# Attention keys in chunks of 128 with shared blocks for the left-over keys, in a fused attention and MLP kernel

## The chip, the cores and the metric

The kernel runs on one core of a Trainium2 chip. The metric is the device time of one execution in microseconds (us); a lower one is better. A run of one kernel is a handful of executions, of which one is profiled.

The engines are called as in the profile: PE is TensorE's matrix multiplies, PEld its weight loads, DVE is VectorE, ACT is ScalarE, POOL is GpSimd, SP is SyncE. POOLq and SPq are the sequencers of the two that issue transfers. L12 is line 12 of the kernel in question, so one piece of work has other line numbers in other kernels. In a row of the profile `x4` is a number of instructions, and what stands in brackets is the time for which the engine stood idle before the row, with what ended that idleness.

## The reference

```python
batch, n_heads, seq, head_dim = (8, 12, 448, 64)      # q, k, v

scores = scale * np.matmul(q, k.transpose(0, 1, 3, 2))
m = np.max(scores, axis=-1, keepdims=True)
e = np.exp(scores - m)
attn = e / (np.sum(e, axis=-1, keepdims=True) + np.exp(-m) + 1e-09)
attn_out = np.matmul(attn, v)

x = attn_out.transpose(0, 2, 1, 3).reshape(B * S, H * D)   # 3584 x 768
h = x @ w_in                                               # w_in: 768 x 2048
g = 0.5 * h * (1.0 + erf(h / sqrt(2)))
return g @ w_out                                           # w_out: 2048 x 768
```

## The kernel before

Two heads form a pair: 6 pairs in each of 8 batches, 48 pairs. The keys of a head (448) are cut in four chunks of 112. For a pair TensorE computes transposed scores, two heads side by side on 64 rows each; ScalarE takes the exponential; VectorE adds the four chunks for the denominators; TensorE multiplies by the values and sums the denominators with a matrix of ones. The MLP of one batch runs between the attention of the next, in units that the steps below are handed.

PSUM, where TensorE's results land, has two buffers of two banks for scores and four single banks for everything else:

```python
re_pool = ctx.enter_context(tc.tile_pool(name="re_pool", bufs=2))
et_pool = ctx.enter_context(tc.tile_pool(name="et_pool", bufs=2))
...
ps_st = ctx.enter_context(tc.tile_pool(name="ps_st", bufs=2, space=bass.MemoryType.PSUM))
ps_bank = ctx.enter_context(tc.tile_pool(name="ps_bank", bufs=4, space=bass.MemoryType.PSUM))
```

The queries and keys must reach TensorE transposed. For batches 2 to 7 a transfer does it. VectorE first copies the loaded rows into a staging buffer `re`, which has two instances here; then a DMA transpose reads it:

```python
def transpose_on_dma(b, w):                       # w: 0 queries, 1 keys
    ...
    re = re_pool.tile([PS, NPAIR, NJ, 2, D], FP16, name="re")
    for e in range(2):
        nc.vector.tensor_copy(out=re[:, :, :, e, :], in_=src[:, :, e])
    nc.sync.dma_start_transpose(out=..., in_=re...)
```

This is a step of the steady part, and what a step fetches (`r` counts the six steps of a batch):

```python
def step(s, first, second):
    closing = s % NPAIR == 0
    if s < NSTEP:
        scores(s, 0)                  # two of four chunks
    for f in first:                   # MLP
        f()
    ...
    if s < NSTEP:
        scores(s, 1)                  # the other two
    if not closing:
        denominators(s - 1)
        values(s - 1)
        reciprocals(s - 1)            # logarithm and exponential on ScalarE
    for f in second:                  # MLP
        f()
    ...
    if not closing:
        normalize(s - 1)              # VectorE

# after each step
if r == 0 and b + 2 < B:
    load_v(b + 2)
if r in (1, 2) and b + 2 < B:
    transpose_on_dma(b + 2, r - 1)
if r == 3 and b + 3 < B:
    load_qk(b + 3)
if r == last:
    gelu_window(b, f1)
```

The loads are issued by GpSimd in program order, each as soon as its buffer is free: `load_v(b + 2)` needs the values of batch b to have been used for the last time, and `load_qk`, which stands behind it in the same queue, waits with it. `gelu_window` runs the rest of layer 1 and all gelus between two loads of ScalarE's tables. MLP results leave their banks through VectorE's copies to `hbuf` and `osb`, or inside the window through ScalarE.

The softmax here doesn't subtract the row's maximum and nothing guards it: scores larger than these inputs give would overflow.

Of the kernel before, what the change touches and what calls it, by code (L numbers as in the profile page):

```python
# [19 lines left out]
def kernel(  # L20
# [16 lines left out]
    PS = S // NJ  # L37
    NPAIR = H // 2
# [16 lines left out]
    re_pool = ctx.enter_context(tc.tile_pool(name="re_pool", bufs=2))  # L55
    qt_pool = ctx.enter_context(tc.tile_pool(name="qt_pool", bufs=2))
    v_pool = ctx.enter_context(tc.tile_pool(name="v_pool", bufs=2))
    et_pool = ctx.enter_context(tc.tile_pool(name="et_pool", bufs=2))
    sum_pool = ctx.enter_context(tc.tile_pool(name="sum_pool", bufs=1))
# [6 lines left out]
    ps_st = ctx.enter_context(tc.tile_pool(name="ps_st", bufs=2, space=bass.MemoryType.PSUM))  # L66
    ps_bank = ctx.enter_context(tc.tile_pool(name="ps_bank", bufs=4, space=bass.MemoryType.PSUM))
# [16 lines left out]
    raw_t, v_t, qt_t = {}, {}, {}  # L84

    def load_heads(pool, name, tiles, key, src, h0=0, h1=H):

        if key not in tiles:
            tiles[key] = pool.tile([PS, H, NJ, D], FP16, name=name)
        nc.gpsimd.dma_start(  # L90
            out=tiles[key][:, h0:h1],
            in_=src[key[0]].rearrange("h (p j) d -> p h j d", j=NJ)[:, h0:h1],
        )

    def load_qk(b, *heads):
        for w, src in (("q", q), ("k", k)):
            load_heads(raw_pool, f"raw{w}", raw_t, (b, w), src, *heads)

    def load_v(b, *heads):
        load_heads(v_pool, "vn", v_t, (b,), v, *heads)  # L100
# [18 lines left out]
    load_qk(0, 0, 2)  # L119
    ident = const.tile([PS, PS], FP16, name="ident")  # L120
    make_identity(nc, ident)
    ones = const.tile([PS, D], FP16, name="ones")
# [6 lines left out]
    load_qk(0, 2, 6)  # L129
    load_v(0, 0, 6)  # L130
    load_qk(0, 6, 12)
    load_v(0, 6, 12)
    load_qk(1)
    for i in range(4):
        load_w_in(i, 4)
    load_v(1)
    for i in range(4):
        load_w_out(i, 4)


    def alloc_qt(b):
        qt_t[b] = qt_pool.tile([P, 2, NPAIR, NJ, PS], FP16, name="tqk")

    def transpose_on_pe(b, c):
        tp = ps_bank.tile([P, 2, NJ, PS], FP16, name="bank")
        for w in range(2):
            src = raw_t[b, "qk"[w]]
            for j in range(NJ):
                for e in range(2):
                    nc.tensor.transpose(  # L150
                        tp[e * D:(e + 1) * D, w, j, :], src[:, 2 * c + e, j, :], ident
                    )
        nc.vector.tensor_copy(out=qt_t[b][:, :, c], in_=tp)  # L153

    def transpose_on_dma(b, w):
        if w == 0:
            alloc_qt(b)
        src = raw_t[b, "qk"[w]].rearrange("p (c e) j d -> p c e j d", e=2)
        re = re_pool.tile([PS, NPAIR, NJ, 2, D], FP16, name="re")
        for e in range(2):  # L160
            nc.vector.tensor_copy(out=re[:, :, :, e, :], in_=src[:, :, e])
        nc.sync.dma_start_transpose(
            out=qt_t[b][:, w].rearrange("p c j s -> p (c j) s"),
            in_=re.rearrange("p c j e d -> p (c j e d)"),
        )


    et_t, sum_t, xt_t = {}, {}, {}

    def scores(g, half):  # L170
        b, c = divmod(g, NPAIR)
        qt, kt = qt_t[b][:, 0], qt_t[b][:, 1]
        if half == 0:
            et_t[g] = et_pool.tile([PS, NJ, 2, S], FP16, name="et")
        for j in (2 * half, 2 * half + 1):
            st = ps_st.tile([P, 2, 512], FP32, name="st")
            for e in range(2):
                r = slice(e * D, (e + 1) * D)
                nc.tensor.matmul(  # L179
                    st[0:PS, e, 0:S], kt[r, c, j, :],  # L180
                    qt[r, c].rearrange("p j s -> p (j s)"), start=True, stop=True,
                )
            nc.scalar.activation(  # L183
                out=et_t[g][:, j], in_=st[0:PS, :, 0:S], func=AF.Exp,
                bias=expb[0:PS], scale=scale,
            )

    def presum(g, part):

        et = et_t[g]  # L190
        if part == 0:
            sum_t[g] = [sum_pool.tile([PS, 2, 2, S], FP16, name="t2"), None]
        t2 = sum_t[g][0]
        nc.vector.tensor_tensor(  # L194
            out=t2[:, part], in0=et[:, 2 * part], in1=et[:, 2 * part + 1], op=ALU.add)
        if part == 1:
            sum_t[g] = sum_pool.tile([PS, 2, S], FP16, name="ksum")
            nc.vector.tensor_tensor(out=sum_t[g], in0=t2[:, 0], in1=t2[:, 1], op=ALU.add)  # L198

    po_t, den_t, rec_t = {}, {}, {}  # L200

    def values(g):
        b, c = divmod(g, NPAIR)
        et = et_t.pop(g)
        po_t[g] = ps_bank.tile([P, 512], FP32, name="bank")
        for j in range(NJ):
            for e in range(2):
                nc.tensor.matmul(  # L208
                    po_t[g][e * D:(e + 1) * D, 0:S], v_t[b,][:, 2 * c + e, j, :], et[:, j, e, :],
                    start=(j == 0), stop=(j == NJ - 1),  # L210
                )

    def denominators(g):
        den_t[g] = ps_bank.tile([P, 512], FP32, name="bank")
        for e in range(2):
            nc.tensor.matmul(  # L216
                den_t[g][e * D:(e + 1) * D, 0:S], ones, sum_t[g][:, e, :], start=True, stop=True,
            )

    def reciprocals(g):  # L220
        rec_t[g] = rec_pool.tile([P, S], FP32, name="rec")
        nc.scalar.activation(out=rec_t[g], in_=den_t.pop(g)[:, 0:S], func=AF.Ln, bias=oneb, scale=1.0)  # L222
        nc.scalar.activation(out=rec_t[g], in_=rec_t[g], func=AF.Exp, scale=-1.0)  # L223
# [8 lines left out]
    def attend(g):  # L232
        denominators(g)
        values(g)
        reciprocals(g)
        normalize(g)

# [3 lines left out]
    NBURST = 10  # L241
# [8 lines left out]
    def layer1(b, fc, direct=False):  # L250
        ph = ps_bank.tile([P, 512], FP32, name="bank")
        for m in range(MCH):
# [3 lines left out]
            )  # L256
        if direct:
# [22 lines left out]
    def layer2_items(b):  # L280
# [7 lines left out]
        for gt, g0, where in tiles:  # L288
            osb_h = {}

            def unit(nh, u, gt=gt, g0=g0, where=where, osb_h=osb_h):
                if nh == 0 and u == 0:
                    osb_h[0] = osb_pool.tile([P, DM], FP32, name="osb")
                if u == 0:
                    osb_h[1] = ps_bank.tile([P, 512], FP32, name="bank")
                osb, po = osb_h[0], osb_h[1]
                n0 = nh * NHW
                for fc in range(u * FCH // 2, (u + 1) * FCH // 2):
# [4 lines left out]
                if u == 0:  # L303
                    return
# [7 lines left out]
            for nh in range(NH):  # L312
                for u in range(2):
                    items.append(lambda nh=nh, u=u, unit=unit: unit(nh, u))
# [6 lines left out]
    def start_step(s):  # L321

        scores(s, 0)
        if s >= 2:
            normalize(s - 2)
        if s + 1 < NPAIR:
            transpose_on_pe(0, s + 1)
        if s >= 1:
            denominators(s - 1)
        presum(s, 0)  # L330
        scores(s, 1)
        if s >= 1:
            values(s - 1)
            reciprocals(s - 1)
        for c in {3: (0,), 4: (1, 2), 5: (3, 4)}.get(s, ()):
            transpose_on_pe(1, c)
        presum(s, 1)

    def step(s, first, second):

        closing = s % NPAIR == 0
        if s < NSTEP:
            scores(s, 0)
        for f in first:
            f()
        if s < NSTEP:
            presum(s, 0)
        if closing:
            attend(s - 1)
        if s < NSTEP:  # L350
            scores(s, 1)
        if not closing:
            denominators(s - 1)
            values(s - 1)
            reciprocals(s - 1)
        for f in second:
            f()
        if s < NSTEP:
            presum(s, 1)
        if not closing:  # L360
            normalize(s - 1)

    def mlp1(b, f0, f1):
        return [lambda fc=fc: layer1(b, fc) for fc in range(f0, f1)]
# [6 lines left out]
    def gelu_window(b, n):  # L371

        load_table(SET_GELU)
        for f in take(len(l2)):
            f()
        if b == 0:
# [13 lines left out]
    transpose_on_pe(0, 0)  # L390
# [3 lines left out]
    load_qk(2)  # L394
    scores(NPAIR, 0)
    normalize(NPAIR - 2)
    transpose_on_pe(1, NPAIR - 1)
    presum(NPAIR, 0)
    denominators(NPAIR - 1)
    values(NPAIR - 1)  # L400
    reciprocals(NPAIR - 1)
    normalize(NPAIR - 1)
    scores(NPAIR, 1)
    for f in mlp1(0, 0, 2):
        f()
    presum(NPAIR, 1)

    for s in range(NPAIR + 1, NSTEP + 1):
        b, r = divmod(s - 1 - NPAIR, NPAIR)

        if b == 0:
            f0, f1, last = 2, 6, 0
        else:
            half = (NBURST if b > 1 else NBURST - 2) // 2
            f0, f1, last = half * r, half * (r + 1), 1
        if r <= last:
            step(s, mlp1(b, f0, f0 + 2), mlp1(b, f0 + 2, f1))
        else:

            left = len(l2) - (0 if b == 0 else 2 if b % 2 == 0 else 4)  # L420
            n = left if r == NPAIR - 1 else max(2, left // (NPAIR - r))
            if r == last + 1:
                n = 4
            step(s, take(n // 2), take(n - n // 2))
        if r == 0 and b + 2 < B:
            load_v(b + 2)
        if r in (1, 2) and b + 2 < B:
            transpose_on_dma(b + 2, r - 1)
        if r == 3 and b + 3 < B:
            load_qk(b + 3)  # L430
        if r == last:
            gelu_window(b, f1)
# [38 lines left out]
```

## Time and profile before

| | before |
|---|---|
| median (lowest to highest), 3 runs | 444.81 us (443.97 to 445.48) |
| profiled span, granted TensorE clock | 442.8 us, 0.995 |
| share busy: PE, ACT, DVE, POOL | 95%, 72%, 45%, 7% |

The prediction shows the main lines of this profile. A timeline gives start, duration, engine, line, operation. The page's row of the TensorE clock has one digit for each fortieth of the span (9 is full speed):

```profile
PEclk9989999999999999999999999999999999999999
```

```profile
123.29 1.02 DVE L161 COPY re<-rawk 112x1536 f16<-112x1536 f16 x2
124.34 3.26 SPq L162 DMA_TRANSPOSE tqk<-re  x1
...
136.04 0.94 POOL L90 DMA_DIRECT2D vn<-in_v_dram  x1 [45.09 <-PE bank L208]
```

VectorE fills the staging buffer without waiting. The second transpose of the batch is issued at 124.34, and the loads of the next values only at 136.04, after both transposes are over. No load runs beside a transpose here (of the twelve in this kernel only the first two, issued together, have any beside them: 296 packets), and in the packets' records a transpose of 2688 packets then lasts 3.4 us, its first packet 1.2 us after the issue.

### The profile page before, as it was taken

To read this page: it belongs to the slowest core of one execution; us is meant where nothing else is said; L and a number is where in the kernel's file an instruction comes from. 1 tells how busy PE (TensorE), PEld (TensorE's weight loads), DVE (VectorE), ACT (ScalarE), POOL (GpSimd) and SP (SyncE) were. 2 spreads that over 40 slices of the span, in tenths; PEclk is the share of its full clock that TensorE was granted. 3 is DMA by queue.
4 is the path that set the end of the run, shared out by engine and by line. 5 is a ranking of instruction groups with operands and counts; after the bars stand their busy time and mean duration, and the time that the engine had idled before them with its cause. 6 is when DMAs were issued, how large, how long until landed. Compare 5 with 4: busy or idle time off the path is not lost.

```text
span 442.8 us, 6605 instructions
## 1 busy us (share of the span) xinstructions
PE 419.7 (95%) x2720; PEld 208.3 (47%) x2720; DVE 198.3 (45%) x351; ACT 317.8 (72%) x426; POOL 32.5 (7%) x43
## 2 busy tenths in 40 slices
PE   3878999999999999999999999999999999999995
PEld 2344444444444454445444454444544455445562
DVE  1567416664165532657154641566346560440021
ACT  3989988978787757969787678887788685854300
POOL 8312100020002000020002000000000000000000
PEclk9989999999999999999999999999999999999999
DMA  8999999696148840493443931460414101111022
GB/s 98 196 207 205 210 199 201 141 164 101 21 99 126 134 98 19 114 145 45 99 98 63 198 60 39 98 99 0 99 44 92 36 1 36 37 36 37 0 73 71
DMA packets 75118, 42.50 MB, mean 96 GB/s; under 512 B 34128, under 2 KB 71504, under 8 KB 75088
## 3 DMA queue, kind: packets, MB, share of 16 engines
q0 software_dynamic: 37968, 22.81, 36.7%
q1 hardware_dynamic: 37120, 19.27, 18.5%
q8 instruction: 21, 0.34, 0.3%
q14 instruction: 9, 0.07, 0.1%
HBM read 45.61 MB, written 11.01 MB: 128 GB/s over the span
## 4 chain that ended last, share of the span: by engine, by line
PE 76%; ACT 17%; issue 2%; DVE 1%; DMA 1%; POOL 1%; POOLq 0%
PE bank L253 34%; PE bank L299 23%; ACT et L183 14%; PE st L179 8%; PE bank L208 8%; PE bank L216 3%; ACT L70 2%; DMA rawk<-in_k_dram 1%; PE bank L150 1%; ACT rec L222 1%; ACT gt_odd L259 0%; ACT gt_even L259 0%; DVE ksum L198 0%; DVE tqk L153 0%; ACT rec L223 0%
## 5 line engine op out<-in xcount | busy, mean ns | idle before, releaser
L183 ACT ACTIVATE et<-st,expb 112x896 f16<-112x896 f32 x192 | 181.5, 1004 | 56.8 <-PE st L179 56.4
L253 PE MATMUL bank<-xt,w_in_sb 128*128 128x448 f16 x768 | 151.2, 353 | 0.0
L305 DVE COPY osb<-bank 128x384 f32<-128x384 f32 x56 | 31.2, 557 | 174.6 <-PE bank L299 174.6
L253 PEld LDWEIGHTS <-w_in_sb 128*128 128x128 f16 x768 | 72.9, 98 | 74.2 <-issue 9.4
L299 PE MATMUL bank<-w_out_sb,gt_odd 128*128 128x384 f16 x512 | 88.0, 326 | 0.0
L179 PE MATMUL st<-tqk 64*112 64x448 f16 x384 | 64.7, 385 | 7.8 <-ACT et L183 5.5
L299 PE MATMUL bank<-w_out_sb,gt_even 128*128 128x384 f16 x384 | 68.5, 327 | 0.0
L299 PEld LDWEIGHTS <-gt_odd 128*128 128x128 f16 x512 | 48.1, 98 | 38.5 <-issue 8.3
L194 DVE TENSOR_TENSOR t<-et 112x896 f16<-112x896 f16 x96 | 59.4, 618 | 5.9 <-ACT et L183 5.3
L263 DVE COPY hbuf<-bank 128x448 f32<-128x448 f32 x64 | 39.9, 624 | 39.0 <-PE bank L253 39.0
L299 PEld LDWEIGHTS <-gt_even 128*128 128x128 f16 x384 | 34.9, 98 | 32.1 <-issue 10.1
L208 PE MATMUL bank<-et,vn 112*64 112x448 f16 x384 | 45.5, 360 | 0.0
L179 PEld LDWEIGHTS <-tqk 64*112 64x112 f16 x384 | 21.7, 127 | 46.4 <-issue 44.5
L259 ACT ACTIVATE gt_odd<-bank 128x448 f16<-128x448 f32 (+1 forms) x64 | 25.3, 401 | 20.2 <-PE bank L253 19.9
L222 ACT ACTIVATE rec<-bank,oneb 128x448 f32<-128x448 f32 x48 | 30.7, 639 | 2.1 <-PE bank L216 2.1
L229 DVE TENSOR_TENSOR xt<-bank,rec 128x448 f16<-128x448 f32 x48 | 29.7, 619 | 5.0 <-ACT rec L223 5.0
L198 DVE TENSOR_TENSOR ksum<-t 112x896 f16<-112x896 f16 x48 | 30.0, 625 | 1.8
L223 ACT ACTIVATE rec<-rec 128x448 f32<-128x448 f32 x48 | 27.7, 577 | 1.5
L208 PEld LDWEIGHTS <-vn 112*64 112x64 f16 x384 | 21.6, 111 | 12.4 <-issue 2.2
L259 ACT ACTIVATE gt_even<-bank 128x384 f16<-128x384 f32 x28 | 13.7, 490 | 17.6 <-PE bank L253 17.6
L90 POOL DMA_DIRECT2D vn<-in_v_dram x9 | 8.1, 903 | 236.4 <-PE bank L208 184.4
L216 PE MATMUL bank<-ksum,ones 112*64 112x448 f16 x96 | 18.5, 380 | 4.5 <-DVE ksum L198 4.5
(24 smaller groups left out, 119.3 us busy)
## 6 DMA issues: line engine op xcount, KB each, us to landing
rawq<-in_q_dram POOLq DMA_DIRECT2D x7, 672.0 KB, 11.7
rawk<-in_k_dram POOLq DMA_DIRECT2D x7, 672.0 KB, 14.1
vn<-in_v_dram POOLq DMA_DIRECT2D x7, 672.0 KB, 8.1
w_in_sb<-in_moe_w_in_dram POOLq DMA_DIRECT2D x4, 768.0 KB, 22.8
w_out_sb<-in_moe_w_out_dram POOLq DMA_DIRECT2D x4, 768.0 KB, 29.9
out_dram<-osb SPq DMA_DIRECT2D x8, 336.0 KB, 2.8
out_dram<-osb SPq DMA_DIRECT2D x8, 288.0 KB, 2.7
out_dram<-osb SPq DMA_DIRECT2D x8, 240.0 KB, 3.3
```

The source lines that it names most:

```text
L179: nc.tensor.matmul(st[0:PS, e, 0:S], kt[r, c, j, :], qt[r, c].rearrange("p j s -> p (j s)"), start=True, stop=True,)
L183: nc.scalar.activation(out=et_t[g][:, j], in_=st[0:PS, :, 0:S], func=AF.Exp, bias=expb[0:PS], scale=scale,)
L194: nc.vector.tensor_tensor(out=t2[:, part], in0=et[:, 2 * part], in1=et[:, 2 * part + 1], op=ALU.add)
L198: nc.vector.tensor_tensor(out=sum_t[g], in0=t2[:, 0], in1=t2[:, 1], op=ALU.add)
L208: nc.tensor.matmul(po_t[g][e * D:(e + 1) * D, 0:S], v_t[b,][:, 2 * c + e, j, :], et[:, j, e, :], start=(j == 0), stop=(j == NJ - 1),)
L216: nc.tensor.matmul(den_t[g][e * D:(e + 1) * D, 0:S], ones, sum_t[g][:, e, :], start=True, stop=True,)
L222: nc.scalar.activation(out=rec_t[g], in_=den_t.pop(g)[:, 0:S], func=AF.Ln, bias=oneb, scale=1.0)
L253: nc.tensor.matmul(ph[:, 0:S], w_in_sb[:, m, fc * P:(fc + 1) * P], xt_t[b][:, m, :], start=(m == 0), stop=(m == MCH - 1),)
L259: nc.scalar.activation(out=dst[:, 0, :], in_=ph[:, c0:c1], func=AF.Gelu)
L263: nc.vector.tensor_copy(out=h_t[b][:, fc, :], in_=ph[:, 0:S])
L299: nc.tensor.matmul(po[:, 0:NHW], gt[:, fc, g0:g0 + P], w_out_sb[:, fc, n0:n0 + NHW], start=(fc == 0), stop=(fc == FCH - 1),)
L305: nc.vector.tensor_copy(out=osb[:, n0:n0 + NHW], in_=po[:, 0:NHW])
```

## The change

Its intent: 448 keys are three chunks of 128 and 64 left over. The left-over keys of the two heads of a pair go into one block-diagonal block of 128 (zeros elsewhere), so that they take one full-array matmul. All row-tiled score matmuls of a pair stand in one burst, the left-over ones in the middle of MLP work that uses the array in full as they do, and the values follow three pairs behind, next to the denominators. This cuts the changes between ways of tiling the array, and work on ScalarE.

```diff
-    re_pool = ctx.enter_context(tc.tile_pool(name="re_pool", bufs=2))
+    left_pool = ctx.enter_context(tc.tile_pool(name="left_pool", bufs=1))
+    re_pool = ctx.enter_context(tc.tile_pool(name="re_pool", bufs=1))
...
-    et_pool = ctx.enter_context(tc.tile_pool(name="et_pool", bufs=2))
-    sum_pool = ctx.enter_context(tc.tile_pool(name="sum_pool", bufs=1))
+    et_pool = ctx.enter_context(tc.tile_pool(name="et_pool", bufs=4))
+    sum_pool = ctx.enter_context(tc.tile_pool(name="sum_pool", bufs=2))
...
-    ps_st = ... bufs=2 ...
-    ps_bank = ... bufs=4 ...
+    ps_st = ... bufs=3 ...
+    ps_bank = ... bufs=2 ...
...
+    def scores_left(g):
+        b, c = divmod(g, NPAIR)
+        qt, _, kl = qt_views(b, c)
+        st = ps_st.tile([P, 2, 512], FP32, name="st")
+        nc.tensor.matmul(st[:, 0, 0:S], kl, qt, start=True, stop=True)
+        exps(g, NK, st)
...
-    def step(s, first, second):
...
+    def step(s, work):
+        if s - 3 in et_t:
+            values(s - 3)                 # left-over values first, full array
+        if s - 2 in sum_t:
+            denominators(s - 2)
+            log_den(s - 2)
+        if s < NSTEP:
+            for j in range(NK):           # NK = 3
+                scores(s, j)
+        if s - 2 in rec_t:
+            exp_den(s - 2)
+        if s - 3 in po_t:
+            normalize(s - 3)
...
+        for i, f in enumerate(work):
+            f(mid=(lambda: scores_left(s)) if i == 0 and s < NSTEP else None)
...
+    def fetch(b, r):
         if r == 0 and b + 2 < B:
             load_v(b + 2)
-        if r in (1, 2) and b + 2 < B:
-            transpose_on_dma(b + 2, r - 1)
+            load_left(vl, v, b + 2)
+        if r in (0, 1) and b + 2 < B:
+            transpose_on_dma(b + 2, r)
         if r == 3 and b + 3 < B:
-            load_qk(b + 3)
+            load_q(b + 3)
+            load_k(b + 3)
+            load_left(kl_raw, k, b + 3)
```

Cut here are the loads in their new shapes (key and value rows as 3 x 64 elements a partition), the sums in six halves instead of three, the start-up in its new order, and the counts of MLP units for each step. `re_pool` goes from two buffers to one, and `fetch` starts the transposes one step earlier.

## The prediction

> **What bounds the kernel now.** I began with the table of engines and the chain that ended last.
>
> ```profile
> span 442.8 us, 6605 instructions
> PE 419.7 (95%) x2720; PEld 208.3 (47%) x2720; DVE 198.3 (45%) x351; ACT 317.8 (72%) x426; POOL 32.5 (7%) x43
> PE 76%; ACT 17%; issue 2%; DVE 1%; DMA 1%; POOL 1%; POOLq 0%
> L183 ACT ACTIVATE et<-st,expb 112x896 f16<-112x896 f32 x192 | 181.5, 1004 | 56.8 <-PE st L179 56.4
> L179 PE MATMUL st<-tqk 64*112 64x448 f16 x384 | 64.7, 385 | 7.8 <-ACT et L183 5.5
> ```
>
> TensorE is the bound, and ScalarE's exponentials (L183) hold it up in places. A busy 95% hides how full the array is, because overlapping records are counted. So I went to the timeline of TensorE in one stretch of steady work.
>
> ```profile
> 199.67 1.86 PE L253 MATMUL bank<-xt,w_in_sb 128*128 128x448 f16 x9
> 201.46 0.58 PE L179 MATMUL st<-tqk 64*112 64x448 f16 x4
> 201.98 0.38 PE L216 MATMUL bank<-ksum,ones 112*64 112x448 f16 x2
> 202.19 0.92 PE L208 MATMUL bank<-et,vn 112*64 112x448 f16 x8
> 203.05 3.58 PE L253 MATMUL bank<-xt,w_in_sb 128*128 128x448 f16 x18
> 206.46 2.76 PE L299 MATMUL bank<-w_out_sb,gt_even 128*128 128x384 f16 x16
> ```
>
> Eighteen L253 matmuls fill 203.05 to 206.46, 189 ns each, and L299 follows at once: both use the full array. But nine of them from 199.67 would end at 201.37, and the scores (L179, two row tiles of 64) start at 201.46, 0.09 late. Scores run two at a time, 0.193 a pair, so four should end at 201.85; the denominators (L216, column tiles) start at 201.98. Eight values (L208) are four pairs of 0.187 and should end at 202.94; L253 starts at 203.05. Every change between full, row-tiled and column-tiled use costs about 0.09 to 0.13 us.
>
> Summing all start-to-start gaps of successive matmuls in the trace gives this account of the span: 4.4 before the first matmul, 378.0 of streaming (189 ns for 448 columns, 163 for 384, a tiled pair counted once), 233 changes of tiling worth 21.9, 32.8 of other waiting, 5.7 after the last start. From 61.1 us to 398.2 (steady work) there are 201 changes (18.9 us) and 14.9 of other waiting, 11.3 of it between one score matmul and the next. Before 40.4 us the other waiting is 17.6. The steps with little MLP work show the score wait:
>
> ```profile
> 180.14 0.59 PE L179 MATMUL st<-tqk 64*112 64x448 f16 x4
> 180.58 3.83 ACT L183 ACTIVATE et<-st,expb 112x896 f16<-112x896 f32 x4 [0.23 <-PE st L179]
> 182.07 0.87 PE L179 MATMUL st<-tqk 64*112 64x448 f16 x4
> 184.30 0.64 ACT L222 ACTIVATE rec<-bank,oneb 128x448 f32<-128x448 f32 x1
> 184.97 0.58 ACT L223 ACTIVATE rec<-rec 128x448 f32<-128x448 f32 x1
> 185.34 0.59 PE L179 MATMUL st<-tqk 64*112 64x448 f16 x4
> ```
>
> The step lasts 5.20 (180.14 to 185.34). The second score burst takes 0.87 where the first takes 0.59, because its score buffer is still being read; ScalarE is nearly full.
>
> **What the Trainium skill says.** "TensorE: Matmul & The Clock Gate" (Wait — 56ns, not 53.3ns?) gives N / 2.4 GHz + 2.5 ns for a warm matmul: 189 for 448, as traced. "TensorEngine Tiling (Array Packing)" (Key Properties) says that changing the tiling mode drains TensorE; the gap of 0.09 agrees. "ScalarE: Activation LUTs" (What ACT_TABLE_LOAD costs) gives 0.833 ns per element with back-to-back overlap: the trace starts successive 896-wide exponentials 906 ns apart, so 448 fewer elements save about 373. "DMA: Bandwidth & Descriptors" (Why small descriptors are slow; Specifications) names about 3 fixed cycles a packet, and a line rate only from 512 B. In this trace packets of 1, 2 and 3 KB read pass an engine every 41, 79 and 117 ns, that is about 3 ns plus 38 per KB; nothing below 512 B written by such loads is in it.
>
> **The change, part by part.**
> Streaming on TensorE does not shrink. A pair's scores were four slots (two heads side by side in each); now they are three such slots and one full-array slot for both left-overs. Values: four slots against one full plus three. Denominators: one. The sum stays at 6 x 1.72 us per batch.
>
> Changes of tiling shrink. Before, a step went MLP, scores, MLP, scores, denominators, values, MLP: five changes. Afterwards it is left-over values (full, like the MLP before them), values and denominators (both column), three score slots (row), MLP; the left-over scores sit inside the MLP and are full. That is three. Forty steady steps x 2 x 0.094 = 7.5 us saved.
>
> ScalarE: four exponentials of 906 become three of 906 and one of about 533; with 667 + 577 for the logarithm and its exponential, 4.87 becomes 4.50 a pair, 18 us in all, most of it where TensorE is the bound anyway.
>
> Score waits: with three score buffers the burst of three needs only buffers that the step before released, so most of the 11.3 us goes. But there are now two other PSUM banks in place of four. I read from the built program what each bank waits for. The first MLP chunk of most steps takes the bank of that step's denominators, once the logarithm has read it. From the denominator's start that is 0.43 to the logarithm (187.26 to 187.69 in the trace), 0.64 for it, 0.05 to react: 1.12. Meanwhile TensorE does the denominators, three score slots and two changes: 0.95. So about 0.17 is newly waited in five steps of six: 33 x 0.17 = 5.6 us. After each of the seven windows of gelu the left-over scores wait for the first exponential behind a 1.28 table load: about 0.5 each, 3.5. Odds and ends, with the last three steps: 3.4. Together 12.5 against 14.9: 2.4 saved. A one-chunk step should go from 5.20 to about 4.80: 0.87 left-over and other values, 0.19, 0.68 of scores, 0.09, 0.17, 2.6 of layer 2, 0.19.
>
> VectorE gets six sums of 448 (or half the partitions) for three of 896. An 896-wide one starts 543 after the last, so fixed time is about 75, and a 448-wide one about 310: 1.86 for 1.63 a pair, 11 us more in all, on an engine that is 45% busy. It lies beside other work unless its copies out of the two banks come late. I find them ready with 0.1 or more to spare.
>
> Start: six pairs at ScalarE's pace, 4.5 for 4.7 to 5, and the first pair hands ScalarE three exponentials before TensorE goes to transpose, so the first MLP matmul (40.4) should come about 2.5 earlier. What takes some back is loading. Key and value rows come in 768 B pieces and left-overs in 256 B, 2304 packets a tensor for 1344. At 3 + 38 per KB that is 3.7 us a tensor for 3.5, 0.9 for the four that stand before the last of w_out.
>
> ```profile
> L114 POOL DMA_DIRECT2D w_out_sb<-in_moe_w_out_dram x4: 742/742/758, 18.0 to 28.7; - x4
> DMA to landing us min/median/max: 29.1/29.9/30.2
> ```
>
> The last quarter of w_out lands at 28.7 + 29.9 = 58.6. Layer 2 started at 61.6; afterwards it would start near 58 to 59 and need that quarter three quarters through, near 60 to 61. I expect a wait of about 1 there, and 0.4 us of values is owed at that point. Start in all: 1.5 saved.
>
> Sum: 7.5 + 2.4 + 1.5 = 11.4 us, so 444.8 - 11.4 = 433.4. End and bare layer 1 and 2 of the last batch (398.2 to 442.8) stay.
>
> **The rivals.**
> First, two banks turn into the new bound: copies by VectorE stand behind sums, or the logarithm comes later than I think. For it: every MLP chunk now has one bank to spare. Against it: a chunk takes 1.14 us and its copy 0.62. If each of 40 steps waits 0.4 rather than 0.17, 9 us are lost, and the time is 442.
> Second, the small writes (384 and 128 B) are much slower than the line through 1, 2 and 3 KB. If the four tensors took twice as long (14 us), w_out would land at 72 and the start would lose about 10: 445. Against it is only the packet arithmetic; nothing in the trace tests it.
> Third, changes of tiling hide more than I count, or ScalarE holds more of the chain than the score waits show (17% of it is ScalarE's). Then the one-chunk steps fall to 4.6 and the start gains 3: 428.
>
> **Range and chances.** The 7.5 is a count and fairly sure. Of the other two terms each could be off by 4 or so, mostly towards less gain, and the start by 3. So 426.5 to 440.5 for eight in ten. The 2% line is 435.9, 2.5 above my figure: 0.68 for faster, 0.29 within, 0.03 slower.
>
> **What would show it.** Right: about 130 changes of tiling from the first layer 2 to the end of attention's overlap; no score matmul waiting for the exponentials except behind a table load; one-chunk steps of 4.8; ScalarE's busy time down by some 15 us or more; TensorE's streaming unchanged at 378. Wrong: VectorE's copies or normalising named as what TensorE waits for, a wait for w_out above 2 us, or software DMA packets whose time does not fall with their size.

## The result, and the profile after

The changed kernel takes 463.94 us (median of 4 runs, 462.89 to 464.96), where the kernel before takes 444.86 (4 runs). It is 4.3% slower: the ratio is 1.043, 95% interval 1.0396 to 1.0465. Ratios are the mean time of one kernel's runs over that of the other's runs of the same rounds, so they need not be quite the ratio of the medians that are quoted. All outputs are right.

The page of the changed kernel, in the places that answer to those shown of before:

```profile
span 463.0 us, 6664 instructions
PE 416.9 (90%) x2612; PEld 212.2 (46%) x2612; DVE 204.6 (44%) x490; ACT 295.7 (64%) x448; POOL 55.2 (12%) x75
PEclk9999999699999999999899997999999999999999
PE 70%; DMA 12%; ACT 10%; DVE 4%; issue 2%; POOL 1%; DVEq 0%; POOLq 0%
L231 ACT ACTIVATE et<-st,expb 128x896 f16<-128x896 f32 x192 | 165.0, 917 | 11.8 <-PE st L241 10.6
```

The change did its own work. ScalarE is busy for 22.1 us less (295.7 against 317.8), and its share of the chain that ended last fell from 17% to 10%. What is new in the chain is a transfer: DMA has 12% of it, and the page puts 11% on the transposes out of `re`. The clock row has slices of 6, 8 and 7: in the trace's clock records TensorE was granted half its speed for 3.4 to 10.2 us from 79.6, 171.8, 226.4 and 281.0 us on, each time at one of the long waits told of below. In e6, the later version without these waits, it was granted in full from 18.3 to 431.3 us.

The view of all waits, with total us, number of times and longest:

```profile
DVE re L215 <- DMA tqk<-re: 37.3, 5, 10.3
PE bank L324 <- DVE osb L378: 12.7, 3, 4.8
PE bank L279 <- DVE xt L306: 8.9, 1, 8.9
```

Five times, once for each of five batches, VectorE's copy into the staging buffer waits for a transpose to have read it, 37.3 us in all. Four times TensorE waits long for VectorE to free one of the banks. The timeline of one such place joins the two (batch 4's queries and keys):

```profile
149.80 1.03 POOL L103 DMA_DIRECT2D vn<-in_v_dram  x1 [41.39 <-PE bank L290]
...
157.26 15.90 SPq L216 DMA_TRANSPOSE tqk<-re  x2
...
161.84 5.36 PE L372 MATMUL bank<-w_out_sb,gt_odd 128*128 128x384 f16 x32
...
169.61 0.83 DVE L215 COPY re<-rawk 128x1152 f16<-128x1152 f16 x2 [6.64 <-DMA tqk<-re]
170.36 1.01 DVE L378 COPY osb<-bank 128x384 f32<-128x384 f32 x2
170.96 5.25 PE L324 MATMUL bank<-xt,w_in_sb 128*128 128x448 f16 x18 [3.75 <-DVE osb L378]
```

It reads from top to bottom. At 149.80 GpSimd gets to issue the loads of the next values, with the next queries and keys behind them: later in the batch's work than before, because the values now lag three pairs and the old ones stay in use for longer. At 157.26 the transpose of the queries is issued, a step earlier than before, and falls among those loads. In the packets' records its first packet comes at 161.34 and its last ends at 169.04. Only then may VectorE refill the single `re` with the keys (169.61). In VectorE's program the copies that empty the two banks of layer 2 come after that copy, so they stand behind its wait until 170.36. Both banks are full, and TensorE waits 3.75. Of the 18 matmuls after it, those that run while the clock is at half (171.78 to 175.19) start 373 ns apart instead of 189: 5.25 us for what should take 3.4.

"DMA: Bandwidth & Descriptors" of the Trainium skill (Issuing engines are not separate DMA queues) says that transfers issued by different engines end on the same 16 DMA engines and interleave. The trace agrees: during those 7.7 us 1815 packets of loads (those of 4 B left out) passed beside the 2688 of the transpose, whose packets took 35 ns on average instead of 21. All five batches with loads beside show bursts of 7.3 to 9.3 us, begun about 4.1 after the issue. The last batch (issue at 325.22) has none left to load; its burst took 3.35, and nobody waited.

What the loss adds up to can be read off the starts of the pairs' first scores. In 42 of 47 gaps the changed kernel is within 0.1 us of the later, mended version of it (e6, 434.4 us, below). In four it is 10.0, 5.6, 6.6 and 6.7 longer, and one after the first is 1.1 longer: 30.1 of the 30.5 us between their spans. The second of the five waits costs nothing, since no layer 2 is ready there and ScalarE empties the banks.

Undisturbed steps look as they were meant to. This is TensorE and ScalarE in a step with one MLP chunk, for the 180.14 to 185.34 of the prediction:

```profile
195.42 0.74 PE L241 MATMUL st<-tqk 64*128 64x448 f16 x6
...
196.06 2.80 ACT L231 ACTIVATE et<-st,expb 128x896 f16<-128x896 f32 x3
...
200.16 0.74 PE L241 MATMUL st<-tqk 64*128 64x448 f16 x6
```

One burst of six score matmuls, no wait inside it, and 4.74 us to the next instead of 5.20.

### The profile page after: what moved, and what is told of

Read it like the earlier page. It is cut to its first block, busy times and chain, and to the rows that moved or that the text cites. A ratio compares the mean times of both kernels' runs of the same rounds, so it can differ in the third digit from the quotient of the medians. Undisturbed runs are those within 1.5% of the kernel's fastest.

```text
span 463.0 us, 6664 instructions
## 1 busy us (share of the span) xinstructions
PE 416.9 (90%) x2612; PEld 212.2 (46%) x2612; DVE 204.6 (44%) x490; ACT 295.7 (64%) x448; POOL 55.2 (12%) x75
## 4 chain that ended last, share of the span: by engine, by line
PE 70%; DMA 12%; ACT 10%; DVE 4%; issue 2%; POOL 1%; DVEq 0%; POOLq 0%
PE bank L324 30%; PE bank L372 26%; DMA tqk<-re 11%; PE bank L282 6%; ACT rec L297 5%; PE bank L290 2%; ACT L72 2%; ACT et L231 2%; PE st L248 2%; PE bank L279 2%; DVE tqk L203 1%; DMA rawk<-in_k_dram 1%; PE st L241 1%; DVE ksum L268 1%; DVE xt L306 1%
## 5 line engine op out<-in xcount | busy, mean ns | idle before, releaser
L231 ACT ACTIVATE et<-st,expb 128x896 f16<-128x896 f32 x192 | 165.0, 917 | 11.8 <-PE st L241 10.6
L324 PE MATMUL bank<-xt,w_in_sb 128*128 128x448 f16 x768 | 156.6, 362 | 13.2 <-DVE osb L378 12.7
L372 PEld LDWEIGHTS <-gt_even 128*128 128x128 f16 x384 | 37.2, 98 | 35.1 <-issue 11.9
L336 DVE COPY hbuf<-bank 128x448 f32<-128x448 f32 x54 | 33.6, 623 | 14.1 <-PE bank L324 12.7
L241 PE MATMUL st<-tqk 64*128 64x448 f16 x288 | 38.7, 369 | 1.1 <-DVE tqk L203 1.1
L282 PE MATMUL bank<-et,vn 128*64 128x448 f16 x288 | 37.5, 370 | 0.0
L268 DVE TENSOR_TENSOR ksum<-ksum,et 64x448 f16<-64x448 f16 x96 | 36.6, 382 | 1.5
L268 DVE TENSOR_TENSOR t<-et 128x448 f16<-128x448 f16 x96 | 33.3, 388 | 2.1 <-ACT et L231 0.6
L268 DVE TENSOR_TENSOR ksum<-t,et 128x448 f16<-128x448 f16 x96 | 33.9, 383 | 0.0
L282 PEld LDWEIGHTS <-vn 128*64 128x64 f16 x288 | 12.4, 110 | 30.4 <-issue 26.6
L279 PE MATMUL bank<-et,vl 128*128 128x448 f16 x48 | 17.3, 361 | 9.0 <-DVE xt L306 8.9
## 6 DMA issues: line engine op xcount, KB each, us to landing
rawq<-in_q_dram POOLq DMA_DIRECT2D x7, 672.0 KB, 10.2
```

The source lines that it names most:

```text
L231: nc.scalar.activation(out=out, in_=in_, func=AF.Exp, bias=expb, scale=scale)
L241: nc.tensor.matmul(st[:, e, 0:S], kt[r, j, :], qt[r], start=True, stop=True)
L268: nc.vector.tensor_tensor(out=dst, in0=a, in1=x, op=ALU.add)
L282: nc.tensor.matmul(po_t[g][e * D:(e + 1) * D, 0:S], v_t[b][:, 2 * c + e, j, :], et[:, 2 * j + e], start=False, stop=(j == NK - 1),)
L324: nc.tensor.matmul(ph[:, 0:S], w_in_sb[:, m, fc * P:(fc + 1) * P], xt_t[b][:, m, :], start=(m == 0), stop=(m == MCH - 1),)
L336: nc.vector.tensor_copy(out=h_t[b][:, fc, :], in_=ph[:, 0:S])
```

## The experiments

Theory A: the transposes of the queries run beside loads, take over twice as long and start later, and the single staging buffer hands that on to VectorE, and VectorE to the banks. The rivals: the single buffer alone costs it; two banks are too few for TensorE whatever the transfers do; the changes of tiling or the lag were not worth what was thought. Runs sent together share the kernel before, whose medians are 445.0 for the first four, 445.4 for the next four and 444.2 for the last four (7 runs each).

| run | edit | median (us) | ratio to before (95%) |
|---|---|---|---|
| after | | 463.94 | 1.043 (1.0396 to 1.0465) |
| e1 | two staging buffers | 441.79 | 0.9927 (0.99 to 0.9955) |
| e2 | transposes a step later | 449.90 | 1.0117 (1.009 to 1.0144) |
| e3 | three exponential tiles for four | 464.46 | 1.0444 (1.0409 to 1.0479) |
| e4 | before, one buffer and early transposes | 453.42 | 1.0195 (1.0168 to 1.0222) |
| e5 | loads held back | 435.97 | 0.9792 (0.9768 to 0.9816) |
| e6 | loads held back, two staging buffers | 434.38 | 0.9758 (0.9742 to 0.9775) |
| e7 | e6, banks split as before | 493.85 | 1.1066 (1.1011 to 1.1121) |
| e8 | e6, burst split again | 447.79 | 1.006 (1.0042 to 1.0077) |
| e9 | e6, left-over scores later | 432.26 | 0.9726 (0.9712 to 0.9741) |
| e10 | e6, values two pairs behind | 447.98 | 1.0072 (1.005 to 1.0094) |
| e11 | before, one buffer | 447.09 | 1.0063 (1.0046 to 1.008) |
| e12 | before, early transposes | 445.01 | 1.0021 (0.9994 to 1.0048) |

### e1_two_bufs and e3_room_only

Two staging buffers do not fit beside four exponential tiles, so e1 takes one of those away, and e3 does that alone.

```diff
 # e1 (e3 has only the second pair of lines)
-    re_pool = ctx.enter_context(tc.tile_pool(name="re_pool", bufs=1))
+    re_pool = ctx.enter_context(tc.tile_pool(name="re_pool", bufs=2))
-    et_pool = ctx.enter_context(tc.tile_pool(name="et_pool", bufs=4))
+    et_pool = ctx.enter_context(tc.tile_pool(name="et_pool", bufs=3))
```

> The changed kernel with two staging buffers for the transposed queries and keys again (and three buffers of exponentials for four, to make room). Theory A: the slowdown is VectorE held, at the keys' copy into the one staging buffer, until the queries' DMA transpose has read it; with two buffers the 37.3 us of VectorE waiting on that transpose go, and with them some 28 us of TensorE waiting: 463.9 - 28 = 436, 433 to 439. Rival B (two PSUM banks as such are too few): the staging buffers do not matter, 460 to 464. Rival C (small-packet loads slow the stretch): 455 or more.

> Control for the first run: the changed kernel with three buffers of exponentials for four and nothing else. Values come first in a step and the scores after them, so the fourth buffer should not be needed: 463 to 465, the same as the changed kernel. If the fourth buffer mattered, slower.

e1 took 441.79 us, 22 less than the changed kernel, though above the 433 to 439 of theory A; e3 took 464.46, as the changed kernel does, so the tile is not what helps. In e1's trace VectorE no longer waits for a transpose. The collision itself is still there, and at the first batch it now shows elsewhere. TensorE's timeline:

```profile
86.88 1.30 PE L241 MATMUL st<-tqk 64*128 64x448 f16 x6 [4.87 <-DMA tqk<-re]
```

The scores of the third batch wait 4.87 us for their keys, and the clock, at half from 85.99 to 92.82, goes with some more: the gaps of that pair and the next are 4.93 and 2.75 longer than in e6, 7.7 together.

### e2_later_transposes

```diff
-        if r in (0, 1) and b + 2 < B:
-            transpose_on_dma(b + 2, r)
+        if r in (1, 2) and b + 2 < B:
+            transpose_on_dma(b + 2, r - 1)
```

> The changed kernel with one staging buffer, but the two transposes one step later, as in the kernel before, when the loads of values, queries and keys have mostly landed. Theory A with its second half (the queries' transpose is slow, 8 us of packets for 3.4, only because it runs beside those loads): the transpose is back to about 3.4 us of packets, VectorE's wait falls under 5 us in all, 435 to 440. If the single buffer is the cause whatever runs beside: still above 450. Rival B: 460 to 464.

It took 449.90 us, which no range had foreseen. Five of the six transposes of the queries came back to 3.4 us, with no loads beside, and the first took 4.9 beside 412 packets of loads. That is theory A's collision nearly gone without another buffer, and VectorE waited for a transpose only once, 3.5 us. But the waits of this kernel have a new row:

```profile
PE st L241 <- DMA tqk<-re: 8.3, 6, 2.5
```

In each of six batches the scores now come before their keys. At these places the gaps between pairs are longer than in e6 by 15 us together, which is the difference of the two kernels. With the values three pairs behind, the MLP of a batch starts a pair later, so a transpose one step later has a step less before it is needed. The early transposes were a necessity of the lag, and the early steps are where the loads were.

### e4_before_one_buf_early, e11_before_one_buf, e12_before_early

The two edits to the fetching, put into the kernel before; e11 has the first alone, e12 the second.

```diff
-    re_pool = ctx.enter_context(tc.tile_pool(name="re_pool", bufs=2))
+    re_pool = ctx.enter_context(tc.tile_pool(name="re_pool", bufs=1))
...
-        if r in (1, 2) and b + 2 < B:
-            transpose_on_dma(b + 2, r - 1)
+        if r in (0, 1) and b + 2 < B:
+            transpose_on_dma(b + 2, r)
```

> The kernel before with what the change did to staging alone: one buffer, and both transposes one step earlier. Here values lag one pair, so the loads are released some two steps earlier relative to the transposes. Theory A: the transposes meet the end of the loads at most, and four PSUM banks give slack: 445 to 449. If the single buffer plus the early transposes are enough by themselves to cost what was seen: 455 to 465.

> The kernel before, with one staging buffer instead of two and nothing else: half of the earlier run with both edits (453.4). Its loads and transposes do not run side by side, and there is a whole step between the two transposes, so by theory A 444 to 447; if the single buffer alone costs 8 us, 452 to 455.

> The kernel before, with its transposes a step earlier and two staging buffers kept: the other half. By theory A the first batch's transposes run beside its loads and the later ones do not, but nobody waits for the buffer: 444 to 448. If the early steps alone cost 8 us, 452 to 455.

Together they cost 8.4 us (453.42 against 445.0), between the two ranges given; alone 2.9 and 0.8, and the interval of the last includes nothing lost. So it is the two in company: an early transpose among loads does harm where VectorE must wait for it. e12 has the same collision (the first two transposes took 16.9 us beside 2634 packets of loads) and no gap grows there, since with two buffers VectorE does not wait. e4's waits:

```profile
DVE re L161 <- DMA rawq<-in_q_dram: 8.7, 1, 8.7
DVE re L161 <- DMA tqk<-re: 8.1, 2, 7.7
```

The first row is a wait for the load of the queries, which e12 has too (9.7 us) without loss. The second is what e4 adds: nearly all of the loss is one gap of 12.55 us at the first batch, for 5.20 in e12 at the same place; the transpose there had 2730 packets of loads beside it and its burst took 12.6. Its later gaps are those of the kernel before to 0.01 us, for there the loads come clear of the transposes even so. The old lag released the loads in another place. So these two edits alone make the collision at the first batch, but not those of the later batches, where 19 of the 30 us lie. That the longer lag put the loads there is read from the times of issue; no run has the changed kernel with the old lag and the loads not held back.

### e5_gated_loads and e6_gated_two_bufs

These change neither buffers (e5) nor transposes, only when the loads are issued. A copy of one element on GpSimd reads the last transposed left-over key, so GpSimd comes to the loads behind it only when that batch's transposes have landed.

```diff
-        if r == 0 and b + 2 < B:
-            load_v(b + 2)
-            load_left(vl, v, b + 2)
         if r in (0, 1) and b + 2 < B:
             transpose_on_dma(b + 2, r)
+        if r == 1 and b + 2 < B:
+            nc.gpsimd.tensor_copy(out=gate, in_=dma_views(b + 2)[2][0:1, NPAIR - 1, P - 1:P])
+            load_v(b + 2)
+            load_left(vl, v, b + 2)
```

Cut here is the line that makes the tile `gate`. e6 has the edits of e1 in addition.

> The changed kernel, staging buffer still single, transposes still in the first two steps; only the issue of the loads of the values two batches ahead (and with them of the queries and keys three ahead) is held back, by a one-element GpSimd copy that reads the last element of the transposed left-over keys, until the batch's transposes have landed. Theory A (the collision of transposes and loads makes the long waits): query transposes back near 3.4 us (were 7.3 to 9.3), first packet about 1.2 us after issue, VectorE's wait for a transpose at the key copy under 2 us instead of 6.6, no long wait of TensorE for VectorE's copies from the third batch on; 433 to 440 us. Rival (the single staging buffer costs it by itself, with loads or without): transposes short, but the waits stay, above 450 us.

> The same with two staging buffers (and three exponential tiles for four, to make room). Theory A: no wait of VectorE for a transpose; the scores of the third batch, which waited 4.9 us for their keys with two buffers and loads beside, start in time; 432 to 438 us, that is 4 to 10 us below the run with two buffers alone (441.8). Rival (loads beside are harmless once there are two buffers, and what remains lies in the start): within 1.5 us of 441.8.

e5 took 435.97 us and e6 434.38. All six transposes of the queries took 3.35 to 3.6 us in both, with no loads beside. In e5 VectorE's waits for `re` fell from 37.3 to 2.7 us with the single buffer that the changed kernel has:

```profile
DVE re L216 <- DMA tqk<-re: 2.7, 2, 1.5
```

That refutes the rival of the single buffer, and shows that the loss needs the collision: without it a second buffer is worth only 1.6 us. In e6 the same place as above reads:

```profile
145.84 9.14 SPq L217 DMA_TRANSPOSE tqk<-re  x2
...
151.37 0.82 DVE L216 COPY re<-rawk 128x1152 f16<-128x1152 f16 x2
...
157.96 0.18 POOL L512 COPY gate<-tqk 1x1 f16<-1x1 f16 x1 [40.95 <-DMA tqk<-klraw]
158.47 1.02 POOL L103 DMA_DIRECT2D vn<-in_v_dram  x1 [0.33 <-issue]
```

Transposes first, then the gate, then the loads; VectorE's copy waits for nothing. The four combinations of buffer and gate make the picture whole: 463.9 (one buffer, no gate), 441.8 (two, none), 436.0 (one, gate), 434.4 (two, gate). The collision costs 28 us with one buffer and 7 with two.

### e7_four_banks

```diff
-    ps_st = ... bufs=3 ...
-    ps_bank = ... bufs=2 ...
+    ps_st = ... bufs=2 ...
+    ps_bank = ... bufs=4 ...
```

> The previous kernel with the split of the accumulator banks of before: two score buffers and four other banks, instead of three and two. Theory A (banks were never the trouble in themselves, only VectorE's late copies): the third score slot waits for the first exponential of the same step, 0.3 us or so in each of 40 steps, and the left-over scores for the second; 3 to 12 us slower than three and two. Rival (two banks tie TensorE to the logarithm and to VectorE): faster than three and two by 3 us or more.

It took 493.85 us, 59 more than e6. The direction is theory A's; the size was misjudged by five times and more. The edit gives up a score buffer for the two banks (both splits use eight in all), so it does not test by itself whether two banks are too few. That rival falls with e5 and e6, which keep two banks: in e6 TensorE's waits for VectorE at a bank, but for the start, are down to 0.6 us. Timeline:

```profile
225.37 2.80 ACT L232 ACTIVATE et<-st,expb 128x896 f16<-128x896 f32 x3
226.42 0.36 PE L242 MATMUL st<-tqk 64*128 64x448 f16 x2 [1.14 <-ACT et L232]
```

The third slot of the burst needs the buffer of the first, whose exponential starts only at 225.37, behind the logarithm of this step's denominators, and takes 0.9. The view of waits has this 44 times, 54.9 us in all, in most steps 1.1 or more. The expectation had left out that the logarithm stands first. The third score buffer is what pays for the burst.

### e8_split_burst

```diff
-            for j in range(NK):
+            for j in range(NK - 1):
                 scores(s, j)
...
-            f(mid=(lambda: scores_left(s)) if i == 0 and s < NSTEP else None)
+            f(mid=(lambda: (scores(s, NK - 1), scores_left(s))) if i == 0 and s < NSTEP else None)
```

> The gated kernel with two staging buffers, with the third score slot moved out of the burst into the middle of the first MLP chunk, next to the left-over scores. It adds two changes of tiling to each of some 40 steps and moves nothing else. If a change of tiling costs its traced 0.09 to 0.13 us on the path: 7.5 to 10 us slower than the unsplit one. If the changes are hidden behind other waits: under 3 us.

It took 447.79 us, 13.4 more than e6, so more than either range. Summing the gaps between matmuls as the prediction does, there are 258 changes of tiling instead of 176, and they cost 24.7 us instead of 16.8: 7.9 for 82, 0.097 each. This figure is no independent measurement, for the sum comes out so only when no change is credited with more than about 0.097 us and the rest is called waiting. What the traces do show is a floor: no change of tiling in the kernel before, e6 or e8 takes less than 0.09 us beyond the streaming, so 82 of them take at least 7.4. The other 6.4 are waits. One is new in the list:

```profile
PE bank L373 <- ACT rec L298: 5.8, 22, 0.7
```

With one slot fewer between the denominators and the first chunk, TensorE comes to the bank before the logarithm has read it. The burst gives the logarithm time as well as saving changes. A one-chunk step takes 5.15 instead of 4.74.

### e9_left_later

After a gelu window the left-over scores wait for a buffer behind ScalarE's table load; they go into the second MLP chunk of such a step.

```diff
-            f(mid=(lambda: scores_left(s)) if i == 0 and s < NSTEP else None)
+            f(mid=(lambda: scores_left(s)) if i == at and s < NSTEP else None)
...
-            step(s, take(n))
+            step(s, take(n), at=1 if b and r == 2 else 0)
```

> The gated kernel with two staging buffers (434.4 us), with the left-over scores of the pair that follows a gelu window moved from the middle of the first MLP chunk into the middle of the second. In six of the seven such steps they waited about 0.63 us (4.45 in all) for a score buffer whose exponential stood behind the table load. If that wait is on the path: 3 to 4 us faster, 430.5 to 431.5. If it is hidden (the time is then lost again at the next bank wait): within 1 us of 434.4.

It took 432.26 us, the fastest of all, though short of the 3 to 4 us expected: 2.1 less than e6 by the medians, 0.3% by the ratios, on another chip. The gap of the six pairs went from 7.78 or 7.73 to 7.24 each, 3.1 us in all. The profiled run lost 1.1 of it again at the first pair, whose loads came later in that run; the traces do not say that the edit caused this. This version beats the kernel before by 2.7%.

### e10_lag_two

```diff
-        if s - 3 in et_t:
-            values(s - 3)
+        if s - 2 in et_t:
+            values(s - 2)
         if s - 2 in sum_t:
             denominators(s - 2)
             log_den(s - 2)
+            exp_den(s - 2)
...
-        if s - 2 in rec_t:
-            exp_den(s - 2)
-        if s - 3 in po_t:
-            normalize(s - 3)
+        if s - 2 in po_t:
+            normalize(s - 2)
```

> The same gated kernel, with the values two pairs behind the scores like the denominators, not three; the logarithm's exponential follows the logarithm at once, and the pair is normalised in the same step. Theory: the lag of three is there because a bank of values must be free again before the second MLP chunk needs it; with two banks and a lag of two, TensorE waits 1 us or more in each of some 40 steps for the normalising VectorE, so 40 to 60 us slower (475 to 495). Rival (the lag buys nothing and only delays the release of the values' buffers): within 4 us of 434.4.

It took 447.98 us, 13.6 more than e6: neither of the two. TensorE hardly waits for VectorE's normalising. In a one-chunk step (4.95 for 4.74) ScalarE's order is what costs:

```profile
186.39 3.31 ACT L232 ACTIVATE et<-st,expb 128x896 f16<-128x896 f32 x4
187.43 0.35 PE L249 MATMUL st<-tqk 128*128 128x448 f16 x1
```

The logarithm's own exponential now goes before the scores' (the group starts 1.26 after the burst at 185.13; in e6 0.64 after it), so the left-over scores at 187.43 get their buffer 0.21 late. By the sum of gaps the left-over scores wait 10.3 us in all for 4.45. And the first chunk, where it is of layer 2, waits more for the logarithm: 9.0 us in all for 2.4. The lag of three is worth keeping, though how much of the 13.6 belongs to the lag and how much to the moved exponential, which the edit needs, was not separated.

## Why the prediction was wrong

It said 433.4 us, 426.5 to 440.5, and gave slower 0.03. The step that failed is the sentence on VectorE, "It lies beside other work unless its copies out of the two banks come late. I find them ready with 0.1 or more to spare." It looked at sums and copies and not at the third thing on that engine, the copies into the staging buffer. It never costed the two edits in the fetching, one staging buffer for two and transposes a step earlier, nor where the longer lag moves the loads. The first rival, "copies by VectorE stand behind sums", named the right engine and the right banks and the wrong cause: they stood behind a transfer. Its stated sign, VectorE's copies named as what TensorE waits for, is what the profile shows. In place of "ready with 0.1 or more to spare" the runs show VectorE held for 37.3 us by five transposes, four of the holds handed on to TensorE, and 30 us lost.

With the loads held back and a second staging buffer (e6) the kernel comes to 434.38 us, 1.0 from the figure predicted. That is partly luck: in the table below the start is off by 1.9 one way and the waits by 1.2 the other. The other steps can be held against that trace:

| term | predicted | e6 against before, by the same sum of gaps |
|---|---|---|
| changes of tiling, steady part | 201 to 130, -7.5 us | 201 to 124, -7.1 |
| other waits, steady part | 14.9 to 12.5, -2.4 | 14.9 to 11.3, -3.6 |
| start | -1.5 | +0.4 to the first layer 2 |
| sum | -11.4 | -10.3 (spans) |

- **Changes of tiling.** Right in number and size: 77 fewer where 40 x 2 = 80 were counted. (80 fewer would leave 121; the "about 130" among the prediction's signs does not fit its own sum.) Each takes 0.09 us or more in the traces. In the changed kernel too it is 201 to 125 and 18.9 to 11.9 us: the gain was had, and the loss came on top of it.
- **Score waits.** Right. The left-over scores behind a table load wait 4.45 us, 3.5 predicted, and e9 shows that they lie on the path. The first chunk's wait for the logarithm is about 3.7 (the rows from score to MLP matmul), 5.6 predicted. The one-chunk step is 4.74, 4.80 predicted.
- **ScalarE.** Busy time fell by 22.1 us; "some 15 or more" was predicted.
- **Start.** Wrong by some 2 us and in its sign. The first MLP matmul comes at 41.9 in e6 and 42.2 in the changed kernel, 40.4 before; 37.9 was predicted. The scores' waits did shrink: up to the first MLP matmul they are 2.8 us by the same sum, 7.7 before. Two things were overlooked that took it back. The starting steps have more changes of tiling, 52 against 32 up to the first layer 2, 1.9 us. And the denominators wait longer for VectorE's sums, the last of which need the left-over exponential: 7.2 us, 4.8 before. Only one of the six opening gaps is near the 4.5 of "ScalarE's pace"; the others are 4.8 to 6.3.
- **Loading.** There was no wait for the last quarter of w_out. The second rival, slow small writes, did not come true: packets of 384 and 128 B written took 53 and 33 ns, where the line through those of 512, 1024 and 1536 B (62, 98 and 135) gives 53 and 35.
- **Third rival.** It did not come true: the one-chunk step is 4.74, not 4.6, and the start lost instead of gaining.

What is left open: the split of e10's 13.6 us, and why a colliding transpose needs 4.1 us to its first packet. That the loads' packets are queued ahead of it fits the records; no run tests it.

## What to carry to other kernels

When a change moves who releases a buffer, follow the buffer to the transfer that fills it and ask what will run beside it: here a lag of two more pairs put loads beside a transpose. Cost each wait of an engine with everything that stands behind it in its program: here a staging copy that waits 7 us holds up two banks and then TensorE. Holding a load back until the urgent transfer has landed can be worth more than a second buffer (436.0 us against 441.8 here), and takes one small instruction.

## What the Trainium skill lacked or had wrong

- "DMA: Bandwidth & Descriptors" (Issuing engines are not separate DMA queues) says that transfers interleave, but neither there nor in its part on the DMA transpose does it say what a transpose pays for it. Here: 3.4 us alone, 7.3 to 9.3 beside 1561 to 2031 packets of loads, and 4.1 instead of 1.2 us from issue to first packet.
- The same page (Specifications) has transfers below 512 B do a read-modify-write. Loads that wrote 384 and 128 B a packet showed no extra time here: 53 and 33 ns a packet, on the line through the larger ones.
- "TensorEngine Tiling (Array Packing)" (Key Properties) says that a change of mode drains TensorE and gives no duration. Here no change took less than 0.09 us beyond the streaming; the medians are 0.094 in the kernel before and 0.096 in e6.
